# Column sums of w_out in two chains on VectorE, mask rows copied from one pair, and another order behind the opening

## The chip, the cores and the metric

The kernel runs on one core of a Trainium2 chip. The metric is device time in microseconds for one execution; the median of three runs of the kernel before is 207.79 us (207.52 to 208.26). The engines of the core work through lists of their own and meet at semaphores: TensorE (PE), VectorE (DVE), ScalarE (ACT), GpSimd (POOL) and SyncE (SP), which here issues nearly all transfers.

## What is computed

A block-sparse attention (4 batches, 8 heads, 768 positions, head size 64) and behind it a two-layer block with a softmax gate and a layer norm.

```python
scores = scale * q @ k.T                       # (4, 8, 768, 768)
mask = band | first/last block | sampled blocks   # on blocks of 32
attn = softmax(where(mask, scores, -1e9)); x = (attn @ v)   # -> (3072, 512)
h = x @ w_in                                   # (3072, 1024)
solu = h * softmax(h)
ln = (solu - mean(solu)) / sqrt(var(solu) + 1e-6) * g_ln
out = ln @ w_out                               # (3072, 512)
```

The kernel folds the mean into the weights: with `wbar` the mean over the 1024 rows of `g_ln * w_out`, `(solu - mean) * g @ w_out` is `solu @ (g * w_out - wbar)`. So it needs the column sums of `g * w_out` before it can write the weights of the last product.

## The kernel before

*Attention.* For each batch b, each third t of the queries (256 rows) and each pair of heads pr, `attend` (L541) makes three groups of four score matmuls (L551) into one of two PSUM tiles `s`, an exp on ScalarE for each (L557) into one of twelve buffers `ex`, 24 matmuls with v (L572) into one of two banks `mbank`, and on VectorE a reciprocal (L581) and a normalisation (L584). The mask comes in through 24 further rows (`MC`) of `kT` and `qT`: 88 rows are contracted, not 64. These rows do not depend on batch or head. There are two sets of `kT` and `qT`. Batch 0 fills set 0 through the opening; L800 and L801 copy the mask rows of all four pairs of set 0 to set 1, once all eight evacuations of k (`kdone`) or of q are done. Later batches write the other 64 rows alone.

*Loads of batches 1 to 3.* Each pair's k, q and v come as f32 into `kst`, `qst`, `vst` (three buffers each), are cast to bf16 (L270 on VectorE or POOL, through `copy`), k and q cross to the other layout by a transposing transfer on SP (L523), and VectorE splits them into `kT` and `qT`.

*Feed.* For each tile of 128 rows `feed` (L618) does two groups of four matmuls with w_in (L631, "feed4"), an exp on ScalarE (L651), a product on VectorE (L654), statistics (L661, L664), a few tiny operations on POOL that end in the scale `rs` (L670, L703), a transposing transfer, two groups of four matmuls with w_out (L748, "out4"), and the scaling on the way out of PSUM (L758), which needs `rs`.

*The weights.* w_in and w_out are loaded as f32 (L399, L410; w_out in two halves `w_out_f` of 1 MB). w_in is cast in eight pieces (L404, "wcast"). For w_out, eight `weigh` (L420, "wg") write `g * w_out` in bf16 to four `ex` buffers, `cs_mm` (L432) sums them over partitions and pieces by eight matmuls of 512 columns with a matrix of ones `onesf`, ScalarE scales the sum to `wbar` (L437), and eight "wo" on VectorE (L439) write the final weights. The first out4 needs four of them.

*The order.* No scheduler runs. Every operation has a number, `ORDER` is a permutation of the 1149 numbers written out by hand, `ENGINES` names the operations that are not on their default engine, and `Plan.run` hands out buffers in that order, oldest free one first. Each engine's list is `ORDER` cut to that engine, and an instruction that waits holds up all behind it on its engine. 26 spare matmuls ("spare512" and smaller) stand between TensorE's work in the opening.

Of the kernel before, what the change touches and what calls it, by code (L numbers as in the profile page):

```python
# [10 lines left out]
ALU = mybir.AluOpType  # L11
# [8 lines left out]
    "ACT": [9, 24, 127, 291, 543, 1070, 1072, 1114, 1118, 1121],  # L20
    "DVE": [89, 92, 93, 95, 96, 126, 134, 135, 143, 161, 162, 165, 389, 393, 412, 420, 622, 626, 630, 639, 653,
        863, 868, 885, 886, 1116],
# [114 lines left out]
def kernel(  # L137
# [11 lines left out]
    nc = tc.nc  # L149
# [265 lines left out]
    wg = []  # L415

    def w_out_g(c):
        return exb[wg[c - c % 2].slot].rearrange("p (a m) t -> p a (m t)", a=2)[:, c % 2, :]

    def weigh(o, c):  # L420
        d, s, k = w_out_g(c), w_out_f[c // 4][:, c % 4, :], g_sb[:, c : c + 1]
        if o.eng == "ACT":
            nc.scalar.mul(out=d, in_=s, mul=k)
        else:
            (nc.vector if o.eng == "DVE" else nc.gpsimd).tensor_scalar(out=d, in0=s, scalar1=k, scalar2=None,  # L425
                                                                       op0=ALU.mult)

    for c in range(KF):
        wg.append(op("wg", "DVE", lambda o, c=c: weigh(o, c), [w_out_load[c // 4], g_cp],
                     take=None if c % 2 else "ex", after=wg[c - 1 :] if c % 2 else ()))  # L430

    def cs_mm(o):  # L432
        for c in range(KF):
            nc.tensor.matmul(mbank[o.slot], onesf, w_out_g(c), start=(c == 0), stop=(c == KF - 1))
# [418 lines left out]
```

## Time and profile before

| what | us |
|---|---|
| median of the runs (range) | 207.79 (207.52 to 208.26) |
| the profiled execution | 206.38 |
| its span, first to last instruction | 204.4 |
| TensorE busy | 198.4 |
| ScalarE busy | 174.0 |
| VectorE busy | 149.9 |
| POOL busy | 58.0 |

The span is what the trace covers; some 2 us of the execution lie outside it. Busy time counts an instruction from its start to its end, and TensorE's overlap, so its share can't be read as work. Rows of a timeline or of a chain begin with the start in us from the start of the span and the duration. A group row ends with busy time and mean duration, and then the idle time before its instructions and who ended it.

### The profile page before, as it was taken

To read this page: it belongs to the slowest core of one execution; us is meant where nothing else is said; L and a number is where in the kernel's file an instruction comes from. 1 tells how busy PE (TensorE), PEld (TensorE's weight loads), DVE (VectorE), ACT (ScalarE), POOL (GpSimd) and SP (SyncE) were. 2 spreads that over 40 slices of the span, in tenths; PEclk is the share of its full clock that TensorE was granted. 3 is DMA by queue.
4 is the path that set the end of the run, shared out by engine and by line. 5 is a ranking of instruction groups with operands and counts; after the bars stand their busy time and mean duration, and the time that the engine had idled before them with its cause. 6 is when DMAs were issued, how large, how long until landed. Compare 5 with 4: busy or idle time off the path is not lost.

```text
span 204.4 us, 5699 instructions
## 1 busy us (share of the span) xinstructions
PE 198.4 (97%) x2269; PEld 141.3 (69%) x2298; DVE 149.9 (73%) x341; ACT 174.0 (85%) x219; POOL 58.0 (28%) x132
## 2 busy tenths in 40 slices
PE   8999999999999999999999999999999999999993
PEld 4689886777657768667767777667677686675452
DVE  3488697999979648959776776599849736686771
ACT  4699999988998999999899899979998997775751
POOL 5705403430133024222303415025040110032160
PEclk9999999999999999999999999999999999999999
DMA  5999999989999999889999989999970921327524
GB/s 141 327 373 362 386 380 265 145 137 246 197 215 322 265 247 228 170 192 256 224 274 228 289 203 275 154 232 228 235 211 5 211 45 32 74 103 157 154 81 180
DMA packets 72214, 43.17 MB, mean 211 GB/s; under 512 B 53316, under 2 KB 67148, under 8 KB 72140
## 3 DMA queue, kind: packets, MB, share of 16 engines
q1 hardware_dynamic: 72152, 42.81, 86.8%
q8 instruction: 18, 0.29, 0.6%
q14 instruction: 8, 0.07, 0.1%
q10 hardware_dynamic: 36, 0.00, 0.0%
HBM read 23.07 MB, written 6.29 MB: 144 GB/s over the span
## 4 chain that ended last, share of the span: by engine, by line
PE 82%; DVE 9%; DMA 4%; issue 1%; POOL 1%; ACT 0%; POOLq 0%; SPq 0%; DVEq 0%
PE s L551 26%; PE mbank L748 17%; PE h L631 15%; PE mbank L572 15%; PE h L464 3%; DMA qx<-qb 2%; DVE us L654 2%; PE h L812 2%; DMA vst<-in_v_dram 2%; DVE w_out_sb L439 1%; PE mbank L812 1%; DVE ots L758 1%; DVE ex L425 1%; PE mbank L771 1%; DVE qT L270 1%
## 5 line engine op out<-in xcount | busy, mean ns | idle before, releaser
L557 ACT ACTIVATE ex<-s 128x1024 bf16<-128x1024 f32 x144 | 141.0, 1025 | 16.1 <-PE s L551 13.8
L551 PE MATMUL s<-qT,kT 88*128 88x256 bf16 x576 | 82.8, 272 | 0.2
L551 PEld LDWEIGHTS <-kT 88*128 88x128 bf16 x576 | 52.8, 97 | 20.9 <-issue 0.5
L748 PE MATMUL mbank<-w_out_sb,uTs 128*128 128x512 bf16 x171 | 45.4, 379 | 0.6
L631 PE MATMUL h<-w_in_sb,xT 128*128 128x512 bf16 x170 | 45.2, 378 | 0.7
L572 PEld LDWEIGHTS <-ex 128*128 128x128 bf16 x1152 | 40.9, 97 | 4.1 <-DVE ots L758 0.5
L572 PE MATMUL mbank<-va,ex 128*128 128x65 bf16 x1152 | 42.3, 193 | 0.3 <-DVE ots L758 0.2
L654 DVE TENSOR_TENSOR us<-h,e 128x1024 bf16<-128x1024 f32 x22 | 26.9, 1221 | 4.5 <-ACT e L651 4.3
L661 DVE BATCH_NORM_STATS2 bs<-us 128x6 f32<-128x512 bf16 x44 | 28.9, 682 | 0.2
L631 PEld LDWEIGHTS <-xT 128*128 128x128 bf16 x192 | 18.5, 97 | 13.9
L748 PEld LDWEIGHTS <-uTs 128*128 128x128 bf16 x184 | 17.3, 97 | 13.1
L758 DVE TENSOR_SCALAR ots<-mbank,rs 128x512 f32<-128x512 f32 x22 | 16.4, 746 | 11.1 <-POOL rs L703 4.5
L651 ACT ACTIVATE e<-h 128x1024 bf16<-128x1024 f32 x22 | 22.6, 1029 | 1.3 <-POOL vr L670 1.3
L581 DVE RECIPROCAL r<-mbank 128x4 f32<-128x4 f32 x48 | 8.1, 172 | 21.1 <-PE mbank L572 20.9
L670 POOL TENSOR_SCALAR vr<-z,mv 128x1 f32<-128x1 f32 x22 | 6.4, 293 | 58.2 <-DVE mv L664 50.5
L584 DVE TENSOR_TENSOR x<-mbank,r 128x256 bf16<-128x256 f32 x48 | 20.1, 421 | 1.2
L703 POOL TENSOR_TENSOR rs<-vr,neg_half 128x1 f32<-128x1 f32 x24 | 13.9, 579 | 1.5
L270 POOL CAST kb<-kst 128x768 bf16<-128x768 f32 x8 | 6.8, 854 | 21.4 <-DMA kst<-in_k_dram 19.8
L270 POOL CAST qb<-qst 128x768 bf16<-128x768 f32 x8 | 6.9, 858 | 11.9 <-DMA qst<-in_q_dram 10.4
L270 POOL CAST va<-vst 128x768 bf16<-128x768 f32 x8 | 6.8, 850 | 11.8 <-DMA vst<-in_v_dram 9.8
L667 POOL TENSOR_TENSOR z<-z 128x1 f32<-128x1 f32 x22 | 4.3, 197 | 19.0 <-ACT e L651 19.0
L270 DVE COPY kT<-kc 64x768 bf16<-64x768 bf16 x24 | 8.3, 348 | 0.6 <-DMA kc<-kb 0.3
(109 smaller groups left out, 133.8 us busy)
## 6 DMA issues: line engine op xcount, KB each, us to landing
vst<-in_v_dram SPq DMA_DIRECT2D x16, 384.0 KB, 4.9
out_dram<-ots SPq DMA_DIRECT2D x23, 256.0 KB, 2.3
kst<-in_k_dram SPq DMA_DIRECT2D x15, 384.0 KB, 5.7
qst<-in_q_dram SPq DMA_DIRECT2D x12, 384.0 KB, 5.6
w_out_f<-in_moe_w_out_dram SPq DMA_DIRECT2D x2, 1024.0 KB, 11.2
qst<-in_q_dram SPq DMA_DIRECT2D x4, 256.0 KB, 7.3
uTs<-in_moe_w_in_dram SPq DMA_DIRECT2D x2, 512.0 KB
ots<-in_moe_w_in_dram SPq DMA_DIRECT2D x2, 512.0 KB, 7.2
```

The lines of the kernel that those rows point to most:

```text
L270: (nc.vector if o.eng == "DVE" else nc.gpsimd).tensor_copy(out=dst, in_=src)
L551: nc.tensor.matmul(s[:, m, :], kT[i][0:KR, pr, jc, hh, :], qT[i][0:KR, pr, 2 * t : 2 * t + 2, hh, :], start=(m % 2 == 0), stop=(m % 2 == 1))
L557: exs.append(op("exp", "ACT", lambda o, so=so: nc.scalar.activation(out=exb[o.slot], in_=lay["s"][so.slot], func=ACT.Exp, scale=scale), [s ...
L572: nc.tensor.matmul(acc(o)[:, qt, hh, :], exb[exs[n].slot][:, m, qt * P : (qt + 1) * P], va[i][:, 2 * pr + hh, jc, :], start=first, stop=(n ...
L584: nrm = op("norm", "DVE", lambda o: nc.vector.tensor_tensor(out=xb[x_of[b, t].slot][:, :, 2 * pr * D : (2 * pr + 2) * D].rearrange("p a (h ...
L631: nc.tensor.matmul(hx(n), xTb[xt[0].slot][:, qt, c, :], w_in_sb[n][:, c, :], start=(c == 0), stop=(c == KD - 1))
L651: zs = op("silu_e", "ACT", lambda o: nc.scalar.activation(out=eb[o.slots["e"]], in_=lay["h"][0].rearrange("p a f -> p (a f)"), func=ACT.Ex ...
L654: us = op("mult", "DVE", lambda o: nc.vector.tensor_mul(out=ub[o.slot], in0=lay["h"][0].rearrange("p a f -> p (a f)"), in1=eb[zs.slots["e" ...
L661: bs.append(op("stats", "DVE", lambda o, n=n: nc.vector.bn_stats(out=bsb[(bs[0] if bs else o).slot][:, n, :], in_=ub[us.slot][:, w(o, n)]) ...
L703: rs = op("rs", "POOL", lambda o: nc.gpsimd.tensor_tensor(out=rsb[o.slot], in0=vrb[vr.slot], in1=neg_half, op=ALU.pow), [vr, c2], take="rs ...
L748: nc.tensor.matmul(mbank[m0.slot], uTb[ut[0].slot][:, KF // 2 * n + f, :], w_out_sb[n][:, f, :], start=(n == 0 and f == 0), stop=(n == 1 a ...
L758: nc.vector.tensor_scalar(out=otb[o.slot], in0=mbank[os_[0].slot], scalar1=rsb[rs.slot], scalar2=None, op0=ALU.mult)
```

## The change

Column sums: `weigh` goes. In its place `gather` runs two chains of four on VectorE, one for each half of w_out: the first step of a chain multiplies a piece by its `g` into `wbar` (f32), the next two add the next piece times its `g` to it, and the fourth writes the chain's sum in bf16 to one half of one `ex` buffer. Two matmuls with `onesf` then sum over partitions. `wbar` holds the running sums first and the mean later.

Mask rows: L800 and L801 copy the rows of pair 0 four times, as 24 x 4 pieces, and wait for pair 0 alone.

Engines and order: sixteen casts go from VectorE to POOL, seven others the other way, one copy of `xT` from ScalarE to VectorE, two output scales from VectorE to ScalarE, and one half scale of the last tile from ScalarE to VectorE. ORDER differs from the ninetieth or so to about the 560th of its 1149 numbers; what follows is the same but for the spare128 that moves.

```diff
-    "ACT": [9, 24, 127, 291, 543, 1070, 1072, 1114, 1118, 1121],
-    "DVE": [89, 92, 93, 95, 96, 126, 134, 135, 143, 161, 162, 165, 389, 393, 412, 420, 622, 626, 630, 639, 653,
-        863, 868, 885, 886, 1116],
+    "ACT": [9, 24, 127, 383, 543, 811, 1070, 1072, 1114, 1121],
+    "DVE": [90, 92, 126, 134, 135, 154, 411, 622, 639, 653, 657, 863, 867, 872, 876, 886, 1116],
 ORDER = [
...
-    wg = []
-
-    def w_out_g(c):
-        return exb[wg[c - c % 2].slot].rearrange("p (a m) t -> p a (m t)", a=2)[:, c % 2, :]
-
-    def weigh(o, c):
-        d, s, k = w_out_g(c), w_out_f[c // 4][:, c % 4, :], g_sb[:, c : c + 1]
...
+    wsum = []
+
+    def colsum():
+        return exb[wsum[KF // 2 - 1].slot].rearrange("p (a m) t -> p a (m t)", a=2)
+
+    def gather(o, c):
+        s, k = w_out_f[c // 4][:, c % 4, :], g_sb[:, c : c + 1]
+        if c % 4 == 0:
+            nc.vector.tensor_scalar(out=wbar, in0=s, scalar1=k, scalar2=None, op0=ALU.mult)
+        else:
+            nc.vector.scalar_tensor_tensor(out=colsum()[:, c // 4, :] if c % 4 == 3 else wbar, in0=s, scalar=k,
+                                           in1=wbar, op0=ALU.mult, op1=ALU.add)
 
     for c in range(KF):
-        wg.append(op("wg", "DVE", lambda o, c=c: weigh(o, c), [w_out_load[c // 4], g_cp],
-                     take=None if c % 2 else "ex", after=wg[c - 1 :] if c % 2 else ()))
+        wsum.append(op("wacc" if c % 4 else "wacc0", "DVE", lambda o, c=c: gather(o, c),
+                       [w_out_load[c // 4], g_cp] + wsum[c - 1 :], take="ex" if c == KF // 2 - 1 else None))
 
     def cs_mm(o):
-        for c in range(KF):
-            nc.tensor.matmul(mbank[o.slot], onesf, w_out_g(c), start=(c == 0), stop=(c == KF - 1))
-
-    cs = op("cs", "PE", cs_mm, wg + [c1], take="m", last_of=wg[::2])
+        for n in range(2):
+            nc.tensor.matmul(mbank[o.slot], onesf, colsum()[:, n, :], start=(n == 0), stop=(n == 1))
+
+    cs = op("cs", "PE", cs_mm, wsum[3::4] + [c1], take="m", last_of=[wsum[KF // 2 - 1]])
...
-            mask1["k"] = op("m1dma", "SP", lambda o: nc.sync.dma_start(out=kT[1][MC], in_=kT[0][MC]), kdone)
-            mask1["q"] = op("m1dma", "SP", lambda o: nc.sync.dma_start(out=qT[1][MC], in_=qT[0][MC]), qdone + [mq0])
+            for nm, t, done in (("k", kT, kdone[:2]), ("q", qT, [qdone[0], qdone[NPR], mq0])):
+                mask1[nm] = op("m1dma", "SP", lambda o, t=t: nc.sync.dma_start(
+                    out=t[1][MC].rearrange("r a c h p -> r a (c h p)"),
+                    in_=t[0][MC, 0:1].rearrange("r a c h p -> r a (c h p)").broadcast_to([NB, NPR, NCH * 2 * P])), done)
```

In the rows below line numbers of the changed kernel are one lower than those of the kernel before. VectorE's list around the column sums, before (L425 are the products with g; L581 and L584 the normalisation of an attention tile; L270 casts and copies; numbers in a tile's name tell its buffer):

```order
L270 COPY xT_104<-mbank_147 128x2x128
L270 CAST w_in_sb_135<-uTs 128x512 x2
L581 RECIPROCAL r_111<-mbank_148 128x4
L584 TENSOR_TENSOR x_100<-mbank_148,r_111 128x2x128
L425 TENSOR_SCALAR ex_91<-w_out_f_139,g_sb 128x512
L425 TENSOR_SCALAR ex_96<-w_out_f_139,g_sb 128x512 x2
L270 CAST w_in_sb_135<-uTs 128x512
L425 TENSOR_SCALAR ex_91<-w_out_f_139,g_sb 128x512
L581 RECIPROCAL r_112<-mbank_147 128x4
L584 TENSOR_TENSOR x_101<-mbank_147,r_112 128x2x128
```

The same place in the changed kernel (L422 and L424 are the steps of the chains):

```order
L269 COPY xT_104<-mbank_148 128x2x128
L424 SCALAR_TENSOR_TENSOR ex_98<-w_out_f_138,g_sb,wbar 128x512
L580 RECIPROCAL r_111<-mbank_147 128x4
L583 TENSOR_TENSOR x_100<-mbank_147,r_111 128x2x128
L580 RECIPROCAL r_112<-mbank_148 128x4
L269 CAST w_in_sb_134<-ots 128x512
L269 COPY xT_104<-mbank_147 128x2x128
L583 TENSOR_TENSOR x_101<-mbank_148,r_112 128x2x128
L422 TENSOR_SCALAR wbar<-w_out_f_139,g_sb 128x512
L424 SCALAR_TENSOR_TENSOR wbar<-w_out_f_139,g_sb,wbar 128x512 x2
L424 SCALAR_TENSOR_TENSOR ex_98<-w_out_f_139,g_sb,wbar 128x512
```

The first half's chain stands ahead of this piece and ends in its second row, the second half's chain is in one block, three w_in casts are gone, and each step of a chain reads what the last one wrote.

POOL's list from the end of the opening to the first k and q of batch 1, before:

```order
L270 CAST qr_86<-qst_72 128x8x64
L270 CAST va_65<-vst_75 128x12x64
L270 CAST w_in_sb_134<-ots 128x512
L270 CAST qr_86<-qst_70 128x8x64
L270 CAST w_in_sb_134<-ots 128x512 x2
L447 MEMSET va_66 128x48
L270 CAST kb_76<-kst_68 128x768
L270 CAST kb_77<-kst_67 128x768
```

and in the changed kernel:

```order
L269 CAST qr_86<-qst_70 128x8x64
L269 CAST va_65<-vst_74 128x12x64
L269 CAST w_in_sb_134<-ots 128x512
L269 CAST w_in_sb_135<-uTs 128x512
L269 CAST w_in_sb_134<-ots 128x512
L269 CAST w_in_sb_135<-uTs 128x512
L269 CAST w_in_sb_134<-ots 128x512
L269 CAST w_in_sb_135<-uTs 128x512
L269 CAST kb_76<-kst_68 128x768
L269 CAST qb_78<-qst_71 128x768
```

Three more w_in casts and the first q cast of batch 1 have come to POOL here, and the v cast is that of the last pair (`vst_74`), where the one of the third pair stood (`vst_75`, now further ahead).

SP's list of transfers behind the first loads, before:

```order
L353 DMA qst_70<-in_q_dram 128x2x256
L399 DMA uTs<-in_moe_w_in_dram 128x2x512
L399 DMA ots<-in_moe_w_in_dram 128x2x512
L353 DMA vst_74<-in_v_dram 128x2x384
L399 DMA ots<-in_moe_w_in_dram 128x2x512
L399 DMA uTs<-in_moe_w_in_dram 128x2x512
L410 DMA w_out_f_139<-in_moe_w_out_dram 128x4x512
L410 DMA w_out_f_138<-in_moe_w_out_dram 128x4x512
```

and in the changed kernel:

```order
L398 DMA uTs<-in_moe_w_in_dram 128x2x512
L409 DMA w_out_f_138<-in_moe_w_out_dram 128x4x512
L352 DMA qst_70<-in_q_dram 128x2x256
L398 DMA ots<-in_moe_w_in_dram 128x2x512
L352 DMA vst_74<-in_v_dram 128x2x384
L398 DMA ots<-in_moe_w_in_dram 128x2x512
L398 DMA uTs<-in_moe_w_in_dram 128x2x512
L409 DMA w_out_f_139<-in_moe_w_out_dram 128x4x512
```

One half of w_out now stands ahead of the last q and v loads of batch 0 and of three w_in loads; the other half keeps the end of the block. Further on, the copy of k's mask rows stands ahead of the first transposing transfer, where it stood behind four of them.

More of the change, by code (lines that the diff above doesn't have):

```diff
@@ L414 @@
     c2 = op("half", "POOL", lambda o: nc.gpsimd.memset(neg_half, -0.5))
-    wg = []
-    def w_out_g(c):
-        return exb[wg[c - c % 2].slot].rearrange("p (a m) t -> p a (m t)", a=2)[:, c % 2, :]
-    def weigh(o, c):
-        d, s, k = w_out_g(c), w_out_f[c // 4][:, c % 4, :], g_sb[:, c : c + 1]
-        if o.eng == "ACT":
-            nc.scalar.mul(out=d, in_=s, mul=k)
-        else:
-            (nc.vector if o.eng == "DVE" else nc.gpsimd).tensor_scalar(out=d, in0=s, scalar1=k, scalar2=None,
-                                                                       op0=ALU.mult)
+    wsum = []
[5 more added lines that the diff above has]
+            nc.vector.tensor_scalar(out=wbar, in0=s, scalar1=k, scalar2=None, op0=ALU.mult)
+        else:
+            nc.vector.scalar_tensor_tensor(out=colsum()[:, c // 4, :] if c % 4 == 3 else wbar, in0=s, scalar=k,
+                                           in1=wbar, op0=ALU.mult, op1=ALU.add)
     for c in range(KF):
-        wg.append(op("wg", "DVE", lambda o, c=c: weigh(o, c), [w_out_load[c // 4], g_cp],
-                     take=None if c % 2 else "ex", after=wg[c - 1 :] if c % 2 else ()))
+        wsum.append(op("wacc" if c % 4 else "wacc0", "DVE", lambda o, c=c: gather(o, c),
+                       [w_out_load[c // 4], g_cp] + wsum[c - 1 :], take="ex" if c == KF // 2 - 1 else None))
     def cs_mm(o):
-        for c in range(KF):
-            nc.tensor.matmul(mbank[o.slot], onesf, w_out_g(c), start=(c == 0), stop=(c == KF - 1))
-    cs = op("cs", "PE", cs_mm, wg + [c1], take="m", last_of=wg[::2])
+        for n in range(2):
+            nc.tensor.matmul(mbank[o.slot], onesf, colsum()[:, n, :], start=(n == 0), stop=(n == 1))
+    cs = op("cs", "PE", cs_mm, wsum[3::4] + [c1], take="m", last_of=[wsum[KF // 2 - 1]])
     wb = op("wbar", "ACT", lambda o: nc.scalar.mul(out=wbar, in_=mbank[cs.slot], mul=1.0 / d_ff), [cs],
```

78 rows, old and new, of the table ORDER are left out of this document.

## The prediction

> **What bounds the kernel now.** I read the page first, then the busy time by stretches, then the waits, and last the chain that ended last.
>
> ```profile
> span 204.4 us, 5699 instructions
> PE 198.4 (97%) x2269; PEld 141.3 (69%) x2298; DVE 149.9 (73%) x341; ACT 174.0 (85%) x219; POOL 58.0 (28%) x132
> ...
> PEclk9999999999999999999999999999999999999999
> ```
>
> TensorE's share of 97% alone is no proof, since its records overlap. Its clock is granted in full in every slice, so it can't be behind a stage.
>
> ```profile
> core 0: us, PE busy (x) PEld busy (x) DVE busy (x) ACT busy (x) POOL busy (x), PEclk, DMA share, GB/s
> 20.00:33.00 13.00, 12.95 (x207) 10.96 (x206) 9.95 (x30) 12.62 (x14) 3.65 (x6) 1.00 1.07 382
> 33.00:43.00 10.00, 9.77 (x126) 7.13 (x127) 9.90 (x18) 9.73 (x14) 3.74 (x5) 1.00 0.99 154
> 43.00:63.00 20.00, 19.63 (x186) 12.95 (x188) 18.39 (x42) 18.05 (x23) 4.65 (x10) 1.00 1.07 218
> ...
> PE mbank L572 <- DVE ots L758: 0.2, 1, 0.2
> ```
>
> The first three rows are the stretch that the change orders anew. TensorE lacks 0.05, 0.23 and 0.37 us there, ScalarE 0.38, 0.27 and 1.95, VectorE 3.05, 0.10 and 1.61: three engines are full at once and only POOL has room. The last row is the one wait behind the opening that TensorE's own list shows; the time lies in its work.
>
> ```profile
> 31.86 2.13 DVE ex L425 x4
> ...
> 36.68 4.81 DMA qx<-qb
> ...
> 52.49 0.66 DVE ots L758
> ...
> 53.26 3.92 DMA vst<-in_v_dram
> 57.21 0.56 DVE va L270
> ...
> 62.03 0.76 DVE ots L758
> ...
> 62.84 0.20 PE mbank L572
> 67.12 0.86 PE h L631 x4
> ```
>
> These pieces of the chain say the same from the other side. From 31.86 to 62.8 it runs over VectorE and the transfers that feed it, and then over TensorE to the end: VectorE's lateness is handed over at 62.84. So work taken from TensorE is worth its full time if VectorE is not later at the points where TensorE needs it.
>
> **The change part by part.** *TensorE.* Eight matmuls over onesf become two.
>
> ```profile
> 33.65 2.07 PE L434 MATMUL mbank<-ex,onesf 128*128 128x512 bf16 x7
> 35.55 0.60 PE L551 MATMUL s<-qT,kT 88*128 88x256 bf16 x4
> ```
>
> From the first of them to the next score lie 1.90 us for eight (one record is missing), 0.24 each; four of the same size in the chain row above take 0.86, 0.215 each. Six fewer: 1.29 to 1.43 us, and I take 1.3. Nothing fills the place, since the 26 spare matmuls are the same in number, and the order in ORDER is old again from about its middle on, so the gain is carried to the end if no wait eats it.
>
> *VectorE, column sums.*
>
> ```profile
> L425 DVE TENSOR_SCALAR ex<-w_out_f,g_sb 128x512 bf16<-128x512 f32 x8 | 4.0, 547 | 0.0
> L439 DVE SCALAR_TENSOR_TENSOR w_out_sb<-w_out_f,g_sb,wbar 128x512 bf16<-128x512 f32 x8 | 6.7, 865 | 0.0
> L425 DVE TENSOR_SCALAR ex<-w_out_f,g_sb x8: 459/480/1047, 27.8 to 33.5; 128x512 bf16<-128x512 f32 x8
> L439 DVE SCALAR_TENSOR_TENSOR w_out_sb<-w_out_f,g_sb,wbar x8: 721/746/1312, 36.6 to 47.6; 128x512 bf16<-128x512 f32 x8
> 27.85 1.27 DVE L425 TENSOR_SCALAR ex<-w_out_f,g_sb 128x512 bf16<-128x512 f32 x3
> ```
>
> Two of the eight stay a tensor_scalar (0.48) and six become a scalar_tensor_tensor, whose nearest row is L439 (0.75): 0.96 + 4.50 = 5.5 us against 4.0, 1.5 more. An accumulation into f32 is not in the trace: at the price of L425 it would be 0 more, at L439's mean 0.87 it would be 2.2 more. I take 1.5, since L439 has the same operation and inputs. Each step reads what the last one wrote; three free ones take 1.27 us, not 1.44, and that overlap (0.08 a step, 0.5 in six) is lost.
>
> *VectorE and POOL, the casts.* Seen from 10 to 65 us:
>
> ```profile
> L270 DVE CAST va<-vst 128x768 bf16<-128x768 f32 x5 | 2.8, 552 | 0.3 <-DMA vst<-in_v_dram 0.3
> L270 DVE CAST w_in_sb<-uTs 128x512 bf16<-128x512 f32 x4 | 1.6, 418 | 0.0
> L270 DVE CAST qr<-qst 128x512 bf16<-128x512 f32 x2 | 0.9, 458 | 0.0
> L270 POOL CAST va<-vst 128x768 bf16<-128x768 f32 x3 | 2.7, 889 | 1.0 <-DMA vst<-in_v_dram 1.0
> L270 POOL CAST w_in_sb<-ots 128x512 bf16<-128x512 f32 x3 | 1.8, 614 | 3.0 <-PE h L464 2.3 <-DMA ots<-in_moe_w_in_dram 0.7
> ```
>
> VectorE gives up four v casts (2.2), two of qr (0.9), four of w_in (1.7), one of q and one of k (0.5 each, taken as a v cast), and takes one of v, one of k (1.1), one of w_in (0.4) and a 0.3 copy of xT from ScalarE: 5.8 - 1.8 = 4.0 less. With the sums it is 2.0 to 2.5 us less over this stretch. POOL gets about four v casts, two qr, four w_in and two more, less three: some 6.5 us, in a stretch where it is idle for most of the time. ScalarE is rid of that 0.4 us copy; later it takes two output scales that VectorE had, off the path where it has room.
>
> *Where POOL's work collides.* This is the cost that isn't on the list.
>
> ```profile
> 31.78 1.42 DVE L425 TENSOR_SCALAR ex<-w_out_f,g_sb 128x512 bf16<-128x512 f32 x2
> 31.86 1.05 POOL L270 CAST kb<-kst 128x768 bf16<-128x768 f32 x1 [8.34 <-DMA kst<-in_k_dram]
> ...
> 36.57 1.98 DVE L439 SCALAR_TENSOR_TENSOR w_out_sb<-w_out_f,g_sb,wbar 128x512 bf16<-128x512 f32 x2
> 36.90 1.10 POOL L270 CAST qb<-qst 128x768 bf16<-128x768 f32 x1 [0.97 <-DMA qst<-in_q_dram]
> ...
> 39.40 0.83 POOL L270 CAST kb<-kst 128x768 bf16<-128x768 f32 x1 [1.41 <-DMA kc<-kb]
> 39.61 1.82 DVE L439 SCALAR_TENSOR_TENSOR w_out_sb<-w_out_f,g_sb,wbar 128x512 bf16<-128x512 f32 x2
> ```
>
> Two L425 alone would take 0.88, two L439 1.41 by the same overlap. Beside a POOL cast they take 0.54, 0.57 and 0.41 longer, and a POOL cast that starts second takes up to 0.27 longer than the 0.83 of the undisturbed one: they go one after the other. POOL is free for 8.34 us before 31.86, and there VectorE ran its casts. In the new order POOL has a v cast, six of w_in and the first k and q cast there (0.83 + 6 x 0.61 + 2 x 0.83 = 6.2 us from about 23.5 to 33), and VectorE six long accumulations, two short ones and a w_in cast (5.9): 12.1 us of work that excludes each other in some 10. The second chain then ends up to 2 us later than it could. The page "SBUF — State Buffer" of the Trainium skill (section "Who interferes with whom") has this as an exclusive lock for VectorE instructions with two SBUF inputs, or in a two-port mode, against a GpSimd instruction that reads SBUF. The rows above agree, and the rule speaks against this change; rival A is what it does at its fullest.
>
> Without collisions the second chain could end at about 32.6 (the second half of w_out is in by about 29.7, an estimate: POOL's cast at 31.86 waits for the second load behind it, and two loads of 0.39 MB take 2.1 us at 382 GB/s; then 0.5 + 3 x 0.8 = 2.9), and TensorE wants it at about 33.3 (L434 starts at 33.65 now, and with the copy gone from ScalarE it can come 0.4 sooner). Of 2 us some 0.7 are covered, so the loss lies between 0 and 1.3; I take 0.6, about the middle.
>
> *Recovered.* 62.84 waits for L758 at 62.03, and that for rs on POOL, which stands behind a v cast at 57.21 that had waited for its transfer. This v cast moves to POOL, so the 0.2 us wait of TensorE goes: -0.2.
>
> *At nothing.* The w_out half loaded early (1 MB, 2.8 us at the 382 GB/s above) makes the last q and v of batch 0 and three w_in loads that much later.
>
> ```profile
> 22.66 0.61 POOL L270 CAST w_in_sb<-ots 128x512 bf16<-128x512 f32 x1 [0.68 <-DMA ots<-in_moe_w_in_dram]
> 29.38 1.03 PE L631 MATMUL h<-w_in_sb,xT 128*128 128x512 bf16 x3
> ```
>
> Now w_in for the first feed is in at 22.6, 6.7 us ahead of it. 2.8 later, and then six casts of 0.61 on POOL: 6.5, just covered; collisions would make the first feeds up to 1 us late, and that lies within A. The mask rows are the same 288 KB, issued sooner and waiting for one pair alone; they cost 0.8 us of a transfer queue, covered since batch 1's first score needs the q transfer of 36.68 anyway. POOL's first rs now stands behind a k and a q cast that wait for loads:
>
> ```profile
> 53.06 0.82 POOL L270 CAST qb<-qst 128x768 bf16<-128x768 f32 x1 [6.95 <-DMA qst<-in_q_dram]
> 56.08 1.03 PE L748 MATMUL mbank<-w_out_sb,uTs 128*128 128x512 bf16 x4
> ```
>
> If that q cast ends at 53.9 as now, rs is there at 54.5 and the scale (52.49 now) at 55.2. The output matmul that needs its bank runs at 56.08: 0.9 us of cover, gone if TensorE is 1.3 us ahead, so up to 0.4 could return there. The last half scale goes to VectorE, beside ScalarE's 0.47 at 201.15: nothing.
>
> **Sum.** -1.3 - 0.2 + 0.6 = -0.9 us. The profiled execution took 206.38 us (span 204.4 and 2.0 around it), and would take 205.5; the median shown is 207.79, 1.4 above it, so 206.9.
>
> **The rivals.** *A, slower: POOL and VectorE block each other.* The chain ends the full 1.3 us late, and in the wo stretch (33 to 48) POOL's four k and q casts meet L439 at 0.41 to 0.57 each, some 2 us; VectorE has 0.10 us idle from 33 to 43, so all of it reaches TensorE through the output matmuls. +1.3 + 2.0 - 1.5 = +1.8: 209.6. It decides once collisions cost more than 1.5 us on that path. For it: three of three overlaps above cost. Against: two of these stand in the old order already, and VectorE has 2 us less to do.
> *B: no collision counts.* -1.5, and a third of a microsecond of the idle 0.65 in the stretch: 206.0.
> *C: no change.* ScalarE is 9.73 of 10 busy up to 43 us and feeds the scores' buffers; then TensorE's 1.3 us turns into waiting for exps, and only the 0.4 us copy taken off ScalarE is gained: 207.4. Against: from 43 to 63 ScalarE has 1.95 us free, where TensorE can use its lead.
>
> **How the numbers follow.** A change below 0.3% (0.62 us) can't be told from none. Forecast 0.36 (206.9, by itself 206.4 to 207.2), A 0.26, B 0.22, C 0.16. Faster is forecast and B, 0.58; same is C, 0.16; slower is A, 0.26. For eight in ten the range goes from just under B to most of A's way, since some of A's collisions are likelier than all: 205.8 to 208.9.
>
> **What would show it.** Right: two L434 matmuls within 0.5 us; their start at 33 to 34; no new row of TensorE waits over 0.3 us from 20 to 63; the chain on TensorE earlier than 62.8; accumulations of about 0.75 with some above 1.1. A: accumulations and L439 means over 1.0, TensorE idle before L434 or the first output matmuls. C: TensorE's idle time up, with ScalarE's exps without gaps. Wrong altogether: a wait for a transfer ahead of the first feeds or of batch 1's first score.

## The result, and the profile after

The changed kernel takes 206.26 us (median of 6 runs, 206.02 to 206.72); the kernel before, run beside it, takes 207.70 (207.04 to 208.26). The ratio is 0.9948 with a 95% interval of 0.9925 to 0.997, so 0.6 to 1.6 us are gained. The forecast was 206.9 and a gain of 0.9. On a second chip the same kernel gave 0.9974 (0.9953 to 0.9995): faster again, by less.

The profiled run of the change took 206.22 us, that of the kernel before 206.38, which lay below all timed runs of that kernel. The two spans alone would therefore hide most of the gain. From the page of the change:

```profile
span 204.2 us, 5675 instructions
PE 197.5 (97%) x2263; PEld 140.9 (69%) x2292; DVE 149.4 (73%) x332; ACT 174.3 (85%) x219; POOL 66.5 (33%) x141
...
PE 90%; DVE 4%; ACT 3%; issue 1%; ACTq 0%
```

POOL is busy for 8.5 us more, VectorE for 0.5 less, although by the prediction's count 4.0 us of casts left it. The busy time by stretches, columns as before:

```profile
20.00:33.00 13.00, 12.77 (x184) 10.46 (x183) 11.50 (x27) 12.63 (x14) 7.75 (x10) 1.00 1.03 352
33.00:43.00 10.00, 9.25 (x147) 7.54 (x147) 9.81 (x19) 9.93 (x14) 4.19 (x6) 1.00 1.07 195
43.00:63.00 20.00, 19.84 (x194) 13.35 (x197) 18.62 (x40) 18.05 (x22) 6.89 (x14) 1.00 1.07 228
```

TensorE now lacks 0.23, 0.75 and 0.16 us, where it lacked 0.05, 0.23 and 0.37. That is 1.14 against 0.65: it idles 0.49 us more. (Where the trace lacks a matmul record some 0.05 us count as idle, about 0.3 us in each of the two sums.) VectorE is as full from 33 to 43 us as before (9.81 of 10).

A stretch that holds the same work in both kernels tells more than the spans. The score matmuls that start at 19.19 us before and at 19.23 in the change (call them A), and those that start at 89.67 and at 88.91 (B), have between them the same TensorE instructions but for eight: six of 512 columns, and two small ones that the new order puts outside the stretch (the transposition of `g`, 0.15 us from its start to the next matmul's, and a spare128, 0.05). From the timelines, before first, then the change (start, duration, work):

```profile
19.19 0.61 PE L551 MATMUL s<-qT,kT 88*128 88x256 bf16 x4
...
89.67 0.60 PE L551 MATMUL s<-qT,kT 88*128 88x256 bf16 x4
```

```profile
19.23 0.61 PE L550 MATMUL s<-qT,kT 88*128 88x256 bf16 x4
...
88.91 0.60 PE L550 MATMUL s<-qT,kT 88*128 88x256 bf16 x4
```

A to B takes 70.48 us before and 69.68 after, 0.80 less. Six matmuls less at 0.215 are -1.29, the two small ones -0.20, the idle time above is +0.49: together -1.00, 0.20 more than was gained. That rest is not shown; it would fit waits that the idle time counts in part only, since the whole gap at a wait is 0.1 to 0.2 us longer than the idle time in it. Behind B the change's execution takes 115.32 us and the other 114.71, so 0.61 of the 0.80 is gone again at the end of the span. No run here tests that part; it took 115.17 in a second execution of the kernel before (e1) and 114.7 to 115.4 in all the others, so it scatters by as much.

The chain that ended last shows where the lateness is handed over now:

```profile
29.76 1.95 ACT ex L556 x2
...
34.39 0.43 PE mbank L433 x2
...
37.11 1.93 DVE w_out_sb L438 x2
...
42.91 1.02 PE mbank L747 x4
...
94.38 0.82 DVE kT L269
```

It is on ScalarE's exps up to 31.7, on TensorE over the two onesf matmuls (0.43 us) to 36.0, on VectorE up to 42.9, and nearly all on TensorE from there to the end; VectorE has it once more from 94.2 to 95.6, over the collided split of the last row. Before, VectorE kept it to 62.84.

### The profile page after: what moved, and what is told of

Same layout as the page of the kernel before. It is cut to its first block, busy times and chain, and to the rows that moved or that the text cites. A ratio compares the mean times of both kernels' runs of the same rounds, so it can differ in the third digit from the quotient of the medians.

```text
span 204.2 us, 5675 instructions
## 1 busy us (share of the span) xinstructions
PE 197.5 (97%) x2263; PEld 140.9 (69%) x2292; DVE 149.4 (73%) x332; ACT 174.3 (85%) x219; POOL 66.5 (33%) x141
## 4 chain that ended last, share of the span: by engine, by line
PE 90%; DVE 4%; ACT 3%; issue 1%; ACTq 0%
PE s L550 29%; PE mbank L747 19%; PE h L630 17%; PE mbank L571 16%; ACT ex L556 3%; PE h L463 2%; PE h L813 2%; DVE w_out_sb L438 2%; PE mbank L813 1%; PE mbank L770 1%; PE s L630 1%; DVE bs L660 1%; DVE kT L269 1%; PE mbank L463 0%; DVE x L583 0%
## 5 line engine op out<-in xcount | busy, mean ns | idle before, releaser
L747 PE MATMUL mbank<-w_out_sb,uTs 128*128 128x512 bf16 x173 | 45.6, 379 | 1.2 <-DVE x L583 0.6
L747 PEld LDWEIGHTS <-uTs 128*128 128x128 bf16 x184 | 17.3, 97 | 13.9 <-issue 0.8
L757 DVE TENSOR_SCALAR ots<-mbank,rs 128x512 f32<-128x512 f32 x20 | 14.9, 746 | 8.4 <-issue 4.3
L583 DVE TENSOR_TENSOR x<-mbank,r 128x256 bf16<-128x256 f32 x48 | 20.1, 420 | 1.1
L269 POOL CAST va<-vst 128x768 bf16<-128x768 f32 x10 | 9.2, 925 | 12.6 <-DMA vst<-in_v_dram 12.5
L269 POOL CAST kb<-kst 128x768 bf16<-128x768 f32 x10 | 8.4, 840 | 11.2 <-DMA kst<-in_k_dram 11.2
L269 POOL CAST qb<-qst 128x768 bf16<-128x768 f32 x9 | 8.2, 915 | 10.3 <-DMA qst<-in_q_dram 10.3
L269 DVE COPY kT<-kc 64x768 bf16<-64x768 bf16 x24 | 10.6, 443 | 0.6 <-DMA kc<-kb 0.2
```

The lines of the kernel that those rows point to most:

```text
L269: (nc.vector if o.eng == "DVE" else nc.gpsimd).tensor_copy(out=dst, in_=src)
L583: nrm = op("norm", "DVE", lambda o: nc.vector.tensor_tensor(out=xb[x_of[b, t].slot][:, :, 2 * pr * D : (2 * pr + 2) * D].rearrange("p a (h ...
L747: nc.tensor.matmul(mbank[m0.slot], uTb[ut[0].slot][:, KF // 2 * n + f, :], w_out_sb[n][:, f, :], start=(n == 0 and f == 0), stop=(n == 1 a ...
L757: nc.vector.tensor_scalar(out=otb[o.slot], in0=mbank[os_[0].slot], scalar1=rsb[rs.slot], scalar2=None, op0=ALU.mult)
```

## The experiments

Twelve kernels ran, in three groups. The kernel before ran beside each group on the same chip (medians 207.09, 206.89 and 206.75), and ratios are to it. The change itself ran in the second group (as f1); with the other two groups it is compared by these ratios, across chips. "A to B" is the stretch above in the one profiled execution of each; the last column has the waits of 0.2 us and more that the view of TensorE's waits shows between 20 and 110 us. That view gives 0.1 to 0.2 us less than the whole gap between two matmuls, which the expectations name.

| kernel | median us | ratio (95%) | A to B | TensorE waits for |
|---|---|---|---|---|
| before | 207.70 | 1 | 70.48 | scale 0.2 |
| e1 before again | 207.50 | 1.0004 (0.9978 to 1.0029) | 71.68 | v cast 0.7, copy of `uTs` 0.5, normalisation 0.3 |
| e2 sums alone | 207.53 | 1.0031 (1.0002 to 1.006) | 72.31 | copy of `uTs` 1.9, last accumulation 1.3 |
| e3 order alone | 207.39 | 1.0007 (0.9986 to 1.0029) | 70.86 | v cast 0.4, split 0.2 |
| e4 old mask copies | 206.77 | 0.9976 (0.9947 to 1.0005) | 70.58 | normalisation 0.5, v cast 0.4, splits 0.4, product 0.2 |
| change | 206.26 | 0.9948 (0.9925 to 0.997) | 69.68 | normalisation 0.6, split 0.2 |
| f1 change again | 206.52 | 0.9974 (0.9953 to 0.9995) | 69.50 | normalisation 0.6, split 0.2 |
| f2 two splits later | 205.79 | 0.9932 (0.9907 to 0.9957) | 70.41 | normalisation 0.6, v cast 0.2, product 0.2 |
| f3 two casts later | 208.44 | 1.0064 (1.0032 to 1.0096) | 71.04 | normalisation 0.7, split 0.2, copy of `xT` 0.2 |
| f4 v loads earlier | 207.47 | 1.0022 (1.0002 to 1.0043) | 71.13 | splits 0.8, normalisation 0.6 |
| g1 normalisation first | 206.00 | 0.9968 (0.9948 to 0.9988) | 69.59 | wo 0.3 |
| g2 g1, split later | 206.14 | 0.997 (0.9949 to 0.9992) | 69.47 | wo 0.2, v cast 0.2 |
| g3 g2, old mask copies | 206.00 | 0.9971 (0.9945 to 0.9996) | 69.64 | wo 0.3, product 0.2 |
| g4 g2, v cast on VectorE | 205.70 | 0.9951 (0.9926 to 0.9976) | 69.29 | wo 0.3 |

### The parts of the change, each alone

*e1* is the kernel before, unchanged.

> The kernel before, unchanged, as a control. The profiled execution of before (206.38 us) lay below all its timed runs (207.04 to 208.26), while that of the change (206.22) lay amid its own. If the spread is one of executions, the ratio is 1.000 within 0.003, and this profile shows what a usual execution loses against the first profile; if the first profile was typical of profiles, this one is near 206.4 again.

Ratio 1.0004. Its profile is worth more: the same code had four waits that its first profile had not.

```profile
PE mbank L572 <- POOL va L270: 0.7, 1, 0.7
PE mbank L572 <- DVE uTs L270: 0.5, 1, 0.5
PE h L464 <- POOL kc L270: 0.4, 1, 0.4
PE mbank L572 <- DVE x L584: 0.3, 1, 0.3
```

The columns are the total, the count and the longest. The third lies in the opening. With one code, A to B took 70.48 and 71.68 us. A wait seen in one execution is a draw, and a comparison of two single profiles is good to about 1 us.

*e2* puts the two chains and two matmuls into the kernel before, at the places and on the engines of the eight products; the half of w_out that lands first is summed first.

```diff
+    SEQ = [4, 5, 6, 7, 0, 1, 2, 3]
+            nc.vector.scalar_tensor_tensor(out=colsum()[:, c // 4, :] if c % 4 == 3 else wbar, in0=s, scalar=k,
+                                           in1=wbar, op0=ALU.mult, op1=ALU.add)
...
-        for c in range(KF):
-            nc.tensor.matmul(mbank[o.slot], onesf, w_out_g(c), start=(c == 0), stop=(c == KF - 1))
+        for n in range(2):
+            nc.tensor.matmul(mbank[o.slot], onesf, colsum()[:, n, :], start=(n == 0), stop=(n == 1))
```

> The kernel before with the two chains and two matmuls, in the old places of the order and on the old engines (the half that lands first is summed first). Theory (the gain is TensorE's 1.3 us less work, and the new order and engines keep VectorE on time): VectorE has 1.5 to 2 us more to do where it is full, so TensorE's gain is lost: from 0.3 us faster to 1 us slower than before. Rival (the sums do not matter, the order and the engines bring the gain): 1 to 2 us slower than before. Rival (the sums bring it whatever the order): 1.0 to 1.4 us faster.

Ratio 1.0031: not faster, and by its interval a little slower. Its timeline shows a reason (L426 are the accumulations, L437 the onesf matmuls; behind the bracket, the wait and who ended it):

```profile
32.00 1.98 DVE L426 SCALAR_TENSOR_TENSOR wbar<-w_out_f,g_sb,wbar 128x512 f32<-128x512 f32 x2
32.07 1.36 POOL L270 CAST kb<-kst 128x768 bf16<-128x768 f32 x1 [8.94 <-DMA kst<-in_k_dram]
34.01 0.75 DVE L426 SCALAR_TENSOR_TENSOR ex<-w_out_f,g_sb,wbar 128x512 bf16<-128x512 f32 x1
34.82 0.59 PE L437 MATMUL mbank<-ex,onesf 128*128 128x512 bf16 x2 [1.34 <-DVE ex L426]
```

TensorE waits 1.34 us for the last accumulation, and that alone is what six matmuls save. The larger wait of the table, 1.9 us for VectorE's copy of `uTs`, follows at 43.58, behind two wo that took 2.54 us; e1 waits 0.5 at this place. One cast of POOL made two accumulations 0.48 longer than 2 x 0.75.

*e3* keeps the order, engines and mask copies of the change and takes the sums back to eight products and eight matmuls.

```diff
-            nc.vector.scalar_tensor_tensor(out=colsum()[:, c // 4, :] if c % 4 == 3 else wbar, in0=s, scalar=k,
-                                           in1=wbar, op0=ALU.mult, op1=ALU.add)
+            (nc.vector if o.eng == "DVE" else nc.gpsimd).tensor_scalar(out=d, in0=s, scalar1=k, scalar2=None,
+                                                                       op0=ALU.mult)
...
-        for n in range(2):
-            nc.tensor.matmul(mbank[o.slot], onesf, colsum()[:, n, :], start=(n == 0), stop=(n == 1))
+        for c in range(KF):
+            nc.tensor.matmul(mbank[o.slot], onesf, w_out_g(c), start=(c == 0), stop=(c == KF - 1))
```

> The changed kernel with the eight products and eight matmuls of before in the places of the chains. Theory (six matmuls less): 1.0 to 1.3 us slower than the change, about 207.4, with 1.9 us between the first of these matmuls and the next score. Rival (order and engines): as fast as the change within 0.3 us, since VectorE has 1.5 us less to do.

Ratio 1.0007: the order alone is worth nothing that can be measured. What the six matmuls cost can be read off directly, in e3 first and then in the change:

```profile
34.20 1.89 PE L433 MATMUL mbank<-ex,onesf 128*128 128x512 bf16 x8
35.93 0.60 PE L550 MATMUL s<-qT,kT 88*128 88x256 bf16 x4
```

```profile
34.22 0.60 PE L433 MATMUL mbank<-ex,onesf 128*128 128x512 bf16 x2
34.66 0.60 PE L550 MATMUL s<-qT,kT 88*128 88x256 bf16 x4
```

From the first onesf matmul to the next score it is 1.73 us against 0.44, 1.29 for six. So the gain needs both: the matmuls that the sums save, and an order in which VectorE can pay for the chains. The change did not run beside e2 and e3; e4, which did and has both, took 206.77 us against 207.53 and 207.39.

*e4* is the change with whole-row copies of the mask rows after all pairs.

```diff
-            for nm, t, done in (("k", kT, kdone[:2]), ("q", qT, [qdone[0], qdone[NPR], mq0])):
...
+            mask1["k"] = op("m1dma", "SP", lambda o: nc.sync.dma_start(out=kT[1][MC], in_=kT[0][MC]), kdone)
+            mask1["q"] = op("m1dma", "SP", lambda o: nc.sync.dma_start(out=qT[1][MC], in_=qT[0][MC]), qdone + [mq0])
```

> The changed kernel with the mask rows copied whole as before, after all pairs. Theory: within 0.3 us of the change; the transfers of k and q bound batch 1, not the mask rows. Rival (smaller pieces and the earlier start bring a part): over 0.5 us slower than the change, with batch 1's first scores waiting.

0.9976 against 0.9948, measured on different chips and with intervals that overlap. The change itself gave 0.9974 on the next chip (f1), so little is left to explain; g3 takes the copies up again.

### Where the collisions are paid

*f1* is the change itself, as a reference for three variants.

> The change as it is, on the chip of the three variants of it that run beside it, as their reference: a ratio of 0.993 to 0.998 to the kernel before. Theory (the gain is six matmuls, 1.1 to 1.3 us, less a few discrete waits of TensorE that differ between executions): the second chain ends when TensorE arrives at the onesf matmuls, so no wait there again; the first out4 again waits 0.6 to 0.8 us for the normalisation behind a split that collided with a POOL cast. Rival (the collisions of the chain itself set the time): TensorE waits for L424 ahead of the onesf matmuls.

The wait at the first out4 came again (0.6), none at the onesf matmuls. In the change's own profile it looks like this (L747 is the first out4, L583 the normalisation that frees its bank, L438 the fourth wo, L269 with `kT` the first split of batch 1):

```profile
40.83 0.73 DVE L438 SCALAR_TENSOR_TENSOR w_out_sb<-w_out_f,g_sb,wbar 128x512 bf16<-128x512 f32 x1
40.93 1.32 POOL L269 CAST qb<-qst 128x768 bf16<-128x768 f32 x1 [2.43 <-DMA qst<-in_q_dram]
...
41.58 0.88 DVE L269 COPY kT<-kc 64x768 bf16<-64x768 bf16 x1
...
42.47 0.38 DVE L583 TENSOR_TENSOR x<-mbank,r 128x256 bf16<-128x256 f32 x1
42.91 1.02 PE L747 MATMUL mbank<-w_out_sb,uTs 128*128 128x512 bf16 x4 [0.64 <-DVE x L583]
```

The cast of q starts 0.1 us after the wo, waits for its end, and then the split waits for the cast: 0.88 where this split takes 0.35 elsewhere. The normalisation stands behind it.

*f2* moves that split behind the normalisation, and one split of batch 2 behind the one that batch 2's first score waits for.

```diff
 L580 RECIPROCAL r_111<-mbank_147 128x4
+L580 RECIPROCAL r_112<-mbank_148 128x4
+L583 TENSOR_TENSOR x_102<-mbank_147,r_111 128x2x128
 L269 COPY kT_62<-kc_80 64x6x128
-L580 RECIPROCAL r_112<-mbank_148 128x4
-L583 TENSOR_TENSOR x_102<-mbank_147,r_111 128x2x128
...
+L269 COPY qT_63<-kc_82 64x6x128
 L269 COPY kT_61<-kc_80 64x6x128
-L269 COPY qT_63<-kc_82 64x6x128
```

> The change with two moves in VectorE's list: the first split of k of batch 1 behind the normalisation that frees the bank of the first out4, and one split of batch 2 behind the split that the first score of batch 2 waits for. Theory (the price of the collisions is paid where a collided split stands ahead of what TensorE waits for): the wait of 0.81 us at the first out4 and that of 0.34 at the first score of batch 2 fall below 0.2 each, TensorE is 0.7 to 1.0 us ahead to the end: 205.2 to 205.7 us, 0.995 to 0.997 of the change. Rival (ScalarE, 9.93 of 10 us busy from 33 to 43, is the bound): the waits come back as waits for exps within 10 us behind, and the time is that of the change within 0.2 us.

The second wait went; the first did not. From its timeline:

```profile
40.86 0.83 POOL L269 CAST qb<-qst 128x768 bf16<-128x768 f32 x1 [2.20 <-DMA qst<-in_q_dram]
40.99 1.24 DVE L438 SCALAR_TENSOR_TENSOR w_out_sb<-w_out_f,g_sb,wbar 128x512 bf16<-128x512 f32 x1
...
42.84 1.02 PE L747 MATMUL mbank<-w_out_sb,uTs 128*128 128x512 bf16 x4 [0.58 <-DVE x L583]
```

Here the cast came first, and the wo ahead of the normalisation paid the 0.5 us. The collision depends on when q's transfer lands; taking away one victim hands it to the next. Nor is the time explained: 0.9932 against f1's 0.9974 on the same chip is 0.7 us by the medians, more than the second wait (0.4 of gap in f1's profile). The intervals of the two just overlap, and g2, which has the second move too, did not repeat it. That part stays open.

*f3* holds POOL's first casts of k and q of batch 1 back behind a tiny operation that waits for the first feed.

```diff
+L666 TENSOR_TENSOR z_126<-z_113 128x1
 L269 CAST kb_76<-kst_68 128x768
 L269 CAST qb_78<-qst_71 128x768
-L666 TENSOR_TENSOR z_126<-z_113 128x1
```

> The change with POOL's first casts of k and q of batch 1 behind a tiny operation that waits for the first feed (34.4 us), so that they no longer lie beside the second chain. Theory (one engine at a time has the store, but TensorE arrived late enough at the onesf matmuls): the two accumulations of 1.19 us fall to 0.74 to 0.80, the second chain ends 0.8 to 0.9 us earlier, and the onesf matmuls start no more than 0.1 us earlier: no gain; the casts then collide with L438 and all transposing transfers of batch 1 come 2 to 4 us later: 206.2 to 207.2 us. Rival (the chain's end sets TensorE's): 0.4 us or more faster than the change. Rival (the accumulations are slow because each reads what the last wrote, not for POOL): they stay at 1.1 to 1.2.

The second chain of the change, with the casts beside it, and below it that of f3:

```profile
30.59 0.99 POOL L269 CAST kb<-kst 128x768 bf16<-128x768 f32 x1 [1.60 <-DMA kst<-in_k_dram]
30.93 2.42 DVE L424 SCALAR_TENSOR_TENSOR wbar<-w_out_f,g_sb,wbar 128x512 f32<-128x512 f32 x2
31.79 1.01 POOL L269 CAST qb<-qst 128x768 bf16<-128x768 f32 x1 [0.21 <-DMA qst<-in_q_dram]
33.38 0.75 DVE L424 SCALAR_TENSOR_TENSOR ex<-w_out_f,g_sb,wbar 128x512 bf16<-128x512 f32 x1
34.22 0.60 PE L433 MATMUL mbank<-ex,onesf 128*128 128x512 bf16 x2
```

```profile
31.91 1.54 DVE L424 SCALAR_TENSOR_TENSOR wbar<-w_out_f,g_sb,wbar 128x512 f32<-128x512 f32 x2
33.49 0.75 DVE L424 SCALAR_TENSOR_TENSOR ex<-w_out_f,g_sb,wbar 128x512 bf16<-128x512 f32 x1
34.97 0.18 DVE L580 RECIPROCAL r<-mbank 128x4 f32<-128x4 f32 x1 [0.73 <-PE mbank L571]
35.21 0.60 PE L433 MATMUL mbank<-ex,onesf 128*128 128x512 bf16 x2
```

Two accumulations fall from 2.42 to 1.54 us, so it is POOL and not the dependence of each step on the last that makes them long. The chain is done at 34.24 and TensorE takes it at 35.21, 0.97 later: VectorE itself then idles 0.73 us waiting for TensorE. (f3's execution is 0.86 us late at A already, from its opening.) Counted from A, the chain ends 0.75 us sooner than in the change, and the onesf matmuls start at 15.12 us against 14.99, no sooner. So the chain's collisions cost nothing where they lie. The whole is 0.9% slower than the change beside it, more than either theory said. Batch 1's first transposing transfer is issued at 36.73 us, in f1 at 31.46; that this makes up the difference is likely but not shown.

*f4* issues v of three pairs ahead of three transposing transfers.

```diff
+L352 DMA vst_73<-in_v_dram 128x2x384
+L352 DMA vst_75<-in_v_dram 128x2x384
+L352 DMA vst_74<-in_v_dram 128x2x384
 L522 DMA_TRANSPOSE kc_81<-kb_77 128x6x128
 L522 DMA_TRANSPOSE kc_82<-qb_79 128x6x128
```

> The change with the loads of v of pairs 1 to 3 of batch 1 issued ahead of three transposing transfers, at 41 us and not at 50 to 57. Theory: the casts of v (57 to 63 us) no longer wait for loads, so the wait of 0.3 to 0.9 us at the first products with v of batch 1 (63 to 65 us), which the change's first profile did not show but those of two neighbours did, can't come: equal to the change or up to 0.5 us faster. Rival: three transfers of 0.39 MB ahead of the transposing ones make the scores or the output of the first feeds late: 0.5 to 2 us slower.

Ratio 1.0022 against 0.9974: the rival was right. The v casts no longer meet a wait of TensorE, but TensorE waits for splits:

```profile
50.65 0.35 DVE L269 COPY qT<-kc 64x768 bf16<-64x768 bf16 x1 [0.78 <-DMA kc<-qb]
...
52.07 0.92 PE L550 MATMUL s<-qT,kT 88*128 88x256 bf16 x7 [0.47 <-DVE qT L269]
```

### Can the wait be removed?

*g1* shortens VectorE's list up to the normalisation, whatever collides: fourth wo, normalisation, statistics, product of the second feed, and then the splits.

```diff
 L269 COPY uTs<-mbank_148 128x1024
-L438 SCALAR_TENSOR_TENSOR w_out_sb_136<-w_out_f_138,g_sb,wbar 128x512
-L660 BN_STATS bs_120<-us 128x6
-L438 SCALAR_TENSOR_TENSOR w_out_sb_136<-w_out_f_138,g_sb,wbar 128x512
-L580 RECIPROCAL r_111<-mbank_147 128x4
+L438 SCALAR_TENSOR_TENSOR w_out_sb_136<-w_out_f_138,g_sb,wbar 128x512 x2
+L580 RECIPROCAL r_111<-mbank_147 128x4
+L583 TENSOR_TENSOR x_102<-mbank_147,r_111 128x2x128
+L660 BN_STATS bs_120<-us 128x6
```

> The change with one reordering on VectorE at 40 to 43 us: the fourth wo, then the normalisation that frees the bank of the first out4, then statistics, the product of the second feed, and only then the two splits of batch 1. Theory (in the last try the normalisation came no earlier because the collision with the cast of q moved from the split to the wo ahead of it, so VectorE's list up to the normalisation has to be shorter, whatever collides): the wait of 0.75 us at the first out4 falls below 0.2, no new one over 0.3 follows at the next feed4; 0.5 to 0.75 us faster than the change: 205.6 to 206.0 us, 0.993 to 0.995 of the kernel before. Rival (three engines are full there, so the wait moves on): a wait of 0.4 to 0.8 us at the next feed4 or score, and the time of the change, 0.9965.

The wait is gone and another stands 5 us behind. From g1's timeline:

```profile
42.30 1.03 PE L747 MATMUL mbank<-w_out_sb,uTs 128*128 128x512 bf16 x4
...
45.29 2.73 DVE L438 SCALAR_TENSOR_TENSOR w_out_sb<-w_out_f,g_sb,wbar 128x512 bf16<-128x512 f32 x4
...
48.07 1.02 PE L747 MATMUL mbank<-w_out_sb,uTs 128*128 128x512 bf16 x4 [0.34 <-DVE w_out_sb L438]
```

and its busy time from 33 to 63 us:

```profile
33.00:43.00 10.00, 10.00 (x152) 7.89 (x151) 9.83 (x18) 9.93 (x14) 4.80 (x7) 1.00 1.13 199
43.00:63.00 20.00, 19.63 (x196) 13.11 (x195) 18.67 (x41) 18.26 (x23) 7.38 (x14) 1.00 1.09 233
```

TensorE is full from 33 to 43 and lacks 0.37 in the next stretch, where the change lacked 0.16. It now waits for the last four wo, which have little room to come sooner on a VectorE that is 9.83 of 10 busy. A to B is 69.59, between the change's 69.68 and 69.50, and 0.9968 is close to f1's 0.9974: the rival was right that the wait moves on, though the new one is smaller than it said and stands before an out4.

*g2* adds f2's second move.

> g1 and the split of batch 2 behind the one that its first score waits for. Theory: also the wait of 0.34 to 0.40 us at 95 us is gone, 0.9 to 1.1 us faster than the change, 0.991 to 0.993 of the kernel before. Rival (the gain of the second try came from the first of its two moves): as g1.

0.997 against g1's 0.9968: nothing. But g1's profile has no wait for that split either, so there was little to win.

*g3* is g2 with e4's mask copies (its diff is above).

> g2 with the copies of the mask rows as in the kernel before (all rows, after all eight evacuations). Theory (the copies are covered): within 0.2 us of g2. Rival (the later copy holds up SP's transposing transfers behind it): 0.4 to 0.6 us slower than g2, as a first comparison hinted (0.9976 against 0.9948 of the kernel before, intervals overlapping).

0.9971 and 0.997, on one chip. The copies are covered, and what e4 hinted at was most likely scatter.

*g4* is g2 with the last v cast of batch 1 on VectorE, behind the normalisations.

```diff
-    "DVE": [90, 92, 126, 134, 135, 154, 411, 622, 639, 653, 657, 863, 867, 872, 876, 886, 1116],
+    "DVE": [90, 92, 126, 134, 135, 154, 411, 420, 622, 639, 653, 657, 863, 867, 872, 876, 886, 1116],
```

> g2 with the last v cast of batch 1 on VectorE, behind the normalisations at 65 us, where on POOL it ran at 62.4 beside VectorE's own v cast. Theory (POOL casts that start when their load lands collide with whatever VectorE runs then): VectorE's v cast takes 0.55 us in place of 0.55 to 1.06, the wait of up to 0.6 us ahead of the products with v at 63 us does not come, equal to g2 or up to 0.4 us faster in the median. Rival (0.55 us more on VectorE shows up later): a wait for a normalisation or a scale between 65 and 75 us, up to 0.5 us slower.

First f2's timeline, which has that cast on POOL, then g4's:

```profile
62.64 0.82 POOL L269 CAST va<-vst 128x768 bf16<-128x768 f32 x1 [1.22 <-DMA vst<-in_v_dram]
...
62.87 1.02 DVE L269 CAST va<-vst 128x768 bf16<-128x768 f32 x1
...
63.94 0.89 PE L571 MATMUL mbank<-va,ex 128*128 128x65 bf16 x24 [0.24 <-DVE va L269]
```

```profile
62.46 1.63 PE L571 MATMUL mbank<-va,ex 128*128 128x65 bf16 x48
62.46 0.55 DVE L269 CAST va<-vst 128x768 bf16<-128x768 f32 x1
```

Without POOL beside it VectorE's cast takes 0.55 and TensorE runs both tiles on end. A to B is the shortest of all, 69.29. The time is 0.9951 of the kernel before, and its interval overlaps both of the change's. So, f2 apart, which stays open, no version comes out ahead of the change.

## Why the prediction was right, and where it was not

**TensorE, -1.3: right.** Two L433 take 0.43 us on the chain, and eight in e3 take 1.29 more. Taking the sums back costs the whole gain, and A to B goes from 69.50 and 69.68 to 70.86. (Of that, 0.4 is e3's v wait, but e3 lacks the wait of 0.6 for the normalisation.)

**Second chain late, +0.6: the mechanism came, its place did not.** The chain ended not at 32.6 but at 34.13, and four of the change's six accumulations took 0.81 to 1.34 us against the 0.74 to 0.75 of a free one:

```profile
L424 DVE SCALAR_TENSOR_TENSOR wbar<-w_out_f,g_sb,wbar x4: 739/1192/1335, 23.1 to 32.2; 128x512 f32<-128x512 f32 x4
L424 DVE SCALAR_TENSOR_TENSOR ex<-w_out_f,g_sb,wbar x2: 752/781/810, 27.2 to 33.4; 128x512 bf16<-128x512 f32 x2
```

But TensorE arrived only then. Its onesf matmuls start at 34.22 with no wait, 0.57 later than the 33.65 of before, because ScalarE's exps set the pace up to 31.7 (the chain above; TensorE waits for an exp at 23.92 and at 31.75). The new order brings it there so late by itself: counted from A the onesf matmuls start at 14.99 us in the change and at 14.87 in e3, which has no chains, against 14.46 before. The prediction had them come 0.4 sooner. The step that failed is "the loss lies between 0 and 1.3; I take 0.6": at this place it is 0, as f3 shows. Two other places paid: 0.18 us more idle time from 20 to 33, and 0.52 more from 33 to 43, most of it the first out4 behind a collided split or wo. Together they are 0.70, close to the 0.6, which is why the total came out: luck, as the prediction priced neither place in this term. The second of them is rival A's mechanism at a third of its price; the first is a small piece of rival C.

**VectorE's balance: missed.** From 10 to 65 us VectorE was to have 2.0 to 2.5 us less to do. It is busy there for 49.49 us against 48.80, and in e1 and f1 for 47.82 and 48.51: 0.7 more each time. So by the prediction's own count collisions took about 3 us more of its time than before (an estimate). The six accumulations took 6.02 us where it had 4.50, and the splits into `kT` have a mean of 443 ns on the page of the change, 348 before. Little of this reached TensorE.

**Recovered, -0.2: right in size, wrong in the reason.** From 43 to 63 TensorE idles 0.16 and not 0.37. But "this v cast moves to POOL, so the wait goes" does not hold. In e3, e4, f2 and g2, all with the new places of the casts, TensorE waits for a v cast at 63.5 to 64.6 us, since POOL's v casts start when their transfers land and double VectorE's own (1.02 above). In g4, with that cast on VectorE, the wait did not come; but the change's own profile has none either, so one profile of g4 does not prove a cure.

**At nothing: right.** No wait for w_in, for the mask copies (g3) or for POOL's first rs is among TensorE's waits in the change.

**What would show it.** Two onesf matmuls within 0.5 us came. Their start at 33 to 34 was missed by 0.2. The chain is on TensorE from 42.9 and not 62.8, sooner than asked. One new wait over 0.3 us (0.64) came, against the forecast. Of rival A's signs the wait at the first out4 came, but the mean of L438 fell from 0.87 to 0.82.

**Against the rivals.** A (209.6) fell since POOL's casts hit wo once, not four times. B (206.0) has the nearest number by the first chip's median; by the second chip's ratio, 0.9974, C's is nearest. B's reason is refuted either way: collisions did count. C (207.4, 0.998 of before) lies outside the interval of the first chip but not of the second. e3 speaks against it: from 20 to 63 us TensorE lacks only 0.24 us there and ScalarE is busy for 40.33 of 43 (40.62 in the change), and six matmuls more lost the gain.

## What to carry to other kernels

Work taken off the bounding engine pays only if its feeders can deliver that much earlier: alone the sums cost 0.3%, alone the order gave nothing, together they gave 0.3 to 0.5%. A collision between two engines is priced by what stands behind its victim, so look for short operations that wait behind a cast whose start depends on a transfer's landing, and not for the longest victims. Compare a stretch that holds the same instructions in several executions before believing a wait from one.

## What had not been expected of the hardware

Short copies from bf16 to bf16 suffer as well: a split of 64x768 takes 0.35 us alone and 0.88 beside a cast of POOL, a delay longer than itself. Order decides who pays: where VectorE's wo was first (40.83, 0.73 us) POOL's cast took 1.32, and where POOL was first (40.86, 0.83) the wo took 1.24. The statistics just ahead of that wo overlap the same cast from 40.86 on, and neither takes longer than alone (0.68 and 0.83):

```profile
40.39 0.68 DVE L660 BATCH_NORM_STATS2 bs<-us 128x6 f32<-128x512 bf16 x1
```

Their group has a mean of 679 ns in the change's page. The Trainium skill's page "SBUF — State Buffer" (section "Who interferes with whom") says the same: the pair of ports goes whole to whichever instruction was issued first, and a VectorE instruction with at most one input there, outside the two-port modes, does not contend. The numbers above agree.
